# Gate projections of the last tile by seven products, with a new written order, in a fused retention and gated FFN kernel

## The chip, the cores and the metric

The kernel runs on one core of a Trainium2 chip. TensorE (PE) multiplies matrices into PSUM; VectorE (DVE), ScalarE (ACT) and GpSimd (POOL) work on rows of 128 partitions; SyncE (SP) issues transfers, and so do POOL and ACT. Each engine takes its own instructions in order and waits on semaphores for the others. The metric is device time in microseconds (us) of one execution, as a median over runs.

## The reference

```python
# retention: q, k, v of shape (4, 8, 768, 64); gamma by head
for t in range(S):
    state = gamma * state + einsum('bhd,bhe->bhde', k[:, :, t], v[:, :, t])
    y[:, :, t] = scale * einsum('bhd,bhde->bhe', q[:, :, t], state)
# x: the heads side by side, (3072, 512); d_ff is 1536
gate = 1 / (1 + exp(-(x @ w_gate)))
val = x @ w_val
out = (gate * val) @ w_out          # (3072, 512)
```

## The kernel before, in words

The sequence is cut into six tiles of 128 steps; tile t holds those steps of all four batches, 512 tokens. A *pair* P (0 to 11) is half a tile, two batches with eight heads each.

**Retention.** For a pair, `load` (line 60) fetches k, q and v through POOL's queue into buffers of four each. Pairs 0 to 3 are turned on PE (`transpose`, 171, its row 178; `turned_out`, 181, copies the result out), pairs 4 to 11 by a transposing transfer that SP issues (`xbar`, 194). `scores` (211) multiplies k and q, `mask` (219) applies the decay on DVE, `inter` (227) and `intra` (236) add the state's and the tile's own part, `y_out` (242) writes the output, transposed, into `xT`. `scaled` (200) makes decayed keys, `state` (256) their product with v. `hold` (555) and `hold_for_sums` (558) are tiny copies on POOL that keep its queue back until a pair's transposes, or a tile's hidden sums, are done. `tile_tables` (148) makes masks and decay tables of the tiles on POOL.

**Feed-forward.** The 1536 hidden columns are 12 chunks of 128, or six groups of two. `up` (297) makes one chunk of gates or values for the 512 tokens by four products of 512 columns; `up_sigmoid` (305) on ACT and `up_finish` (310) on DVE make the hidden values `hT`. Tile 1 uses halves of 256 tokens and two chunks (`up_half`, 313).

**Seven products instead of eight.** A group of two chunks, two halves of tokens and two halves of the inner dimension is a 2 x 2 by 2 x 2 block product. `half_product` (365) does it by seven block products instead of eight, each of two instructions of 256 columns, with sums of weight blocks (`ws` or `gws`) and of token blocks (`xs`, made by `x_sums`, 343, on DVE). The running sum of a bank is copied out by ACT midway (`val_copy`), and DVE adds the finished rest (`val_add`); `val_finish` multiplies with the gates on POOL and DVE. Values use this for most groups of tiles 3 and 4 and for all of tile 5. Gates do not use it in the order before, though `gate_copy`, `gate_add` and `gate_sigmoid` (412 to 427) are written. The down projection with `w_out` uses seven products too: `weight_sums` (434), `hidden_sums` (450, on DVE), `product` (464), `fast_copy`, `fast_add`, `fast_store`. `halves_sums` (333) makes the weight sums of a group by four POOL instructions, `late_weight_sums` (353) does so late, in a buffer that a load of q or k has left: before, for the sixth group of values alone.

**The order.** The kernel is scheduled by hand. `STEPS` (618) gives each step a two-letter name, and `ORDER` (678) is a list of six strings of steps, one a tile; a `+` or `-` shifts the step's tile, and a step in capitals uses the whole array in one instruction where small letters use two half-width ones (`mm`, 282). Each engine gets its instructions in this order. Names used below: `gm`, `vm` a chunk of gates or values; `gp`, `vp` one of the seven products for gates or values (first digit the group, second the product); `dw` a late weight sum (number: four times the group, plus which of the four); `hs` a hidden sum; `tp` a transposition on PE; `lk`, `lq`, `lv` loads; `xk`, `xq` turning transfers; `sc` scores; `dp` one of the seven down products. What stands ahead of `ORDER` (lines 567 to 616: the tables, pairs 0 and 1, the first chunk, and the loads up to pair 5) is issued first.

PSUM has seven banks for everything but the state (`bank`, 163). Where a buffer is taken again, the framework makes the new writer wait for the last reader.

Of the kernel before, what the change touches and what calls it, by code (L numbers as in the profile page):

```python
# [13 lines left out]
ALU = mybir.AluOpType  # L14
# [3 lines left out]
def kernel(  # L18
# [10 lines left out]
    nc = tc.nc  # L29
# [250 lines left out]
    gated = {}  # L280
# [84 lines left out]
    def half_product(t, g, n, which):  # L365
        lo, hi = (slice(i * 128, (i + 1) * 128) for i in (2 * g, 2 * g + 1))
        w, sums = ((wg, gws.get(g)), (wv, ws[:, g] if g < 5 else gws.get(6)))[which]
        mine = pairs.setdefault((t, g, which), {})
        if (n == 2) not in mine:
            mine[n == 2] = bank([128, 512])  # L370
        a = b = mine[n == 2][:, :256]
        c = mine[n == 2][:, 256:]
        for kk in range(KT // 2):
            s = lambda i: sums[:, i, kk]
            own = lambda k0, cols: w[:, k0 + kk, cols]
            x = lambda k0, c0: xT[t][:, k0 + kk, c0:c0 + 256]
            to, left, right = {
                1: lambda: (a, own(0, lo), x(0, 0)),
                2: lambda: (b, own(2, lo), x(2, 0)),
                3: lambda: (c, s(3), x(2, 256)),  # L380
                4: lambda: (a, own(2, hi), xs[t][:, 3, kk]),
                5: lambda: (c, s(0), xs[t][:, 0, kk]),
                6: lambda: (a, s(1), xs[t][:, 1, kk]),
                7: lambda: (a, s(2), xs[t][:, 2, kk]),
            }[n]()
            mm(t, to, left, right, start=(kk == 0 and n in (1, 2)), stop=(kk == KT // 2 - 1))

    def val_copy(t, g, n):
        ac = pairs[t, g, 1][0]
# [20 lines left out]
            nc.vector.tensor_tensor(h[:, 2 * g + 1, :256], s[:, :256], pairs[t, g, 1][0][:, :256], op=ALU.mult)  # L410

    def gate_copy(t, g, n):
        ac = pairs[t, g, 0][0]
        lo, hi = sigmoids(t, 2 * g), sigmoids(t, 2 * g + 1)
        o, x = {1: (lo[:, :256], ac[:, :256]), 5: (hi[:, 256:], ac[:, 256:]), 6: (lo[:, 256:], ac[:, 256:])}[n]
        nc.scalar.copy(o, x)

    def gate_add(t, g, n):
        ac, b = pairs[t, g, 0][0], pairs[t, g, 0].get(1)
        lo, hi = gated[t, 2 * g], gated[t, 2 * g + 1]  # L420
        o, x = {5: (lo[:, :256], b), 6: (lo[:, 256:], ac), 7: (hi[:, 256:], ac)}[n]
        nc.vector.tensor_tensor(o, o, x[:, :256], op=ALU.add)

    def gate_sigmoid(t, g, n):
        s = gated[t, 2 * g + (n != 6)]
        o, x = {6: (s, s), 7: (s[:, 256:], s[:, 256:]), 4: (s[:, :256], pairs[t, g, 0][0][:, :256])}[n]
        nc.scalar.activation(o, x, AX.Sigmoid)

    wt = wpool.tile([128, 4, NFF // 2, 256], BF16, name="wt")
# [183 lines left out]
    for s in range(4):  # L613
# [62 lines left out]
    }  # L676
    STEPS.update({n.upper(): f for n, f in STEPS.items()})
    ORDER = [
# [53 lines left out]
    ]  # L732
    for t, order in enumerate(ORDER):
        for s in order.split():
# [34 lines left out]
```

## Time and profile before

| what | value |
|---|---|
| median of 3 runs | 221.43 us (221.16 to 224.9) |
| span of the profiled execution, first to last instruction | 219.1 us |
| what lies around the span, median less span | 2.3 us |
| mean granted clock of TensorE | 0.992 |
| bytes moved by DMA | 25.35 MB |
| out stores on SP | 22 of 256 KB, 3.5 us to landing |

The profile was taken on one execution. A page lists busy times by engine, the chain of waits that ended last, and groups of instructions by line, with the mean duration of one and the idle time ahead of it. PE's durations overlap, since products are pipelined, so the spacing of their starts is read from the timeline. `PE position` in the text is the start of a step, if PE worked from 18.7 us on without waiting, by the spacing of the products ahead of it in the order. A row of DMA issues gives the microseconds from issue to landing.

### The profile page before, as it was taken

What the parts mean: (1) busy time and instruction counts of PE and PEld (TensorE: products, weight loads), DVE (VectorE), ACT (ScalarE), POOL (GpSimd) and SP (SyncE); (2) the same over time, 40 slices, a digit from 0 to 9 for tenths busy, and PEclk for the clock granted to TensorE, in tenths of its full rate; (3) what the DMA queues carried; (4) which work ended last, traced back from release to release, by engine and by line L of the source; (5) the groups of instructions that cost most, each with busy time, mean ns of one, the idle gap of its engine ahead of it and who ended that gap; (6) DMA issues with size and microseconds to landing.
All of it is one profiled execution on the core that took longest, in us unless ns stands there. A gap on an engine that the chain in (4) does not pass through costs nothing.

```text
span 219.1 us, 6849 instructions
## 1 busy us (share of the span) xinstructions
PE 209.3 (96%) x2900; PEld 161.2 (74%) x2906; DVE 158.3 (72%) x330; ACT 115.8 (53%) x254; POOL 131.6 (60%) x149
## 2 busy tenths in 40 slices
PE   6678999999999999999999999999999999999993
PEld 6454455889878866787689776789877867787782
DVE  6764877977448797978797688688768686474871
ACT  7484276425684373752738845635266537345431
POOL 8977786779388994699057834550083670427700
PEclk9889999999999999999999999999999999999999
DMA  9999999999991999999994999800121000022014
GB/s 127 142 171 195 192 176 159 193 191 157 144 138 51 112 183 166 167 140 152 118 215 74 180 198 168 118 0 3 57 85 56 3 1 3 0 96 79 22 46 149
DMA packets 103999, 25.35 MB, mean 116 GB/s; under 512 B 93984, under 2 KB 101152, under 8 KB 103968
## 3 DMA queue, kind: packets, MB, share of 16 engines
q0 software_dynamic: 81248, 13.90, 83.5%
q1 hardware_dynamic: 22576, 10.88, 26.6%
q8 instruction: 22, 0.36, 0.7%
q10 hardware_dynamic: 144, 0.13, 0.2%
q14 instruction: 9, 0.07, 0.1%
HBM read 28.31 MB, written 6.29 MB: 158 GB/s over the span
## 4 chain that ended last, share of the span: by engine, by line
PE 95%; DVE 2%; ACT 1%; issue 1%
PE ff L288 54%; PE ff L284 28%; PE ff L216 4%; PE ff L239 2%; PE ff L178 2%; PE ff L233 2%; PE ff L531 2%; PE z L261 1%; DVE qkT L188 1%; ACT xT L252 0%; DVE qn L572 0%; DVE xT L252 0%; ACT qkT L188 0%; DVE lgp L117 0%; ACT ob L504 0%
## 5 line engine op out<-in xcount | busy, mean ns | idle before, releaser
L308 ACT ACTIVATE gs<-ff 128x512 f32<-128x512 f32 (+1 forms) x61 | 35.2, 591 | 28.3 <-PE ff L288 17.0
L288 PE MATMUL ff<-xT,wg 128*64 128x512 bf16 (+1 forms) x408 | 47.3, 363 | 0.0
L405 POOL TENSOR_TENSOR hT<-gs,scr 128x512 bf16<-128x512 f32 x17 | 21.9, 1292 | 33.9 <-DVE scr L399 19.0
L288 PE MATMUL ff<-xT,wv 128*64 128x256 bf16 (+1 forms) x352 | 35.6, 324 | 0.0
L288 PEld LDWEIGHTS <-wg 128*64 128x64 bf16 x408 | 22.8, 110 | 11.5
L221 DVE TENSOR_TENSOR st<-ff,maskd 128x512 bf16<-128x512 f32 x40 | 25.8, 684 | 6.7 <-PE ff L216 6.6
L288 PEld LDWEIGHTS <-wv 128*64 128x64 bf16 x388 | 21.5, 110 | 7.8 <-issue 0.2
L399 DVE TENSOR_TENSOR scr<-scr,ff 128x256 f32<-128x256 f32 x51 | 20.4, 416 | 9.1 <-PE ff L284 3.5
L284 PE MATMUL ff<-xT,wg 128*128 128x256 bf16 (+1 forms) x131 | 24.3, 321 | 1.8 <-ACT xT L252 0.9
L311 DVE TENSOR_TENSOR hT<-gs,ff 128x512 bf16<-128x512 f32 (+1 forms) x27 | 17.6, 663 | 9.3 <-PE ff L288 3.9
L514 DVE TENSOR_TENSOR ob<-p,ff 128x256 f32<-128x256 f32 x33 | 13.6, 417 | 12.6 <-ACT p L506 5.5
L288 PEld LDWEIGHTS <-hT 128*64 128x64 bf16 x372 | 20.2, 110 | 2.5
L209 ACT ACTIVATE kt<-kn,tabk 128x128 bf16<-128x128 bf16 x48 | 16.9, 395 | 8.0 <-DVE hT L328 5.8
L408 POOL TENSOR_TENSOR hT<-gs,scr 128x256 bf16<-128x256 f32 x17 | 12.8, 758 | 11.3 <-DVE scr L399 8.7
L284 PEld LDWEIGHTS <-wg 128*128 128x128 bf16 x136 | 13.1, 98 | 7.7 <-issue 0.9
L254 DVE TENSOR_TENSOR xT<-ff,taby 128x512 bf16<-128x512 f32 x20 | 13.5, 686 | 3.7 <-PE ff L239 3.7
L392 ACT COPY scr<-ff 128x512 f32<-128x512 f32 x17 | 9.8, 585 | 11.8 <-PE ff L288 6.8
L288 PE MATMUL ff<-wo,hT 128*64 128x256 bf16 (+1 forms) x204 | 15.7, 292 | 0.0
L64 POOL DMA_DIRECT2D vn<-in_v_dram x12 | 14.0, 1170 | 2.4 <-DMA wo<-in_moe_w_out_dram 0.8
L284 PE MATMUL ff<-xT,wv 128*128 128x256 bf16 (+1 forms) x96 | 15.5, 290 | 0.0
L64 POOL DMA_DIRECT2D kn<-in_k_dram x11 | 13.0, 1181 | 2.7 <-PE ff L216 1.7
L288 PEld LDWEIGHTS <-hs 128*64 128x64 bf16 x252 | 13.7, 110 | 0.7
(108 smaller groups left out, 413.1 us busy)
## 6 DMA issues: line engine op xcount, KB each, us to landing
out_dram<-ob SPq DMA_DIRECT2D x22, 256.0 KB, 3.5
vn<-in_v_dram POOLq DMA_DIRECT2D x12, 256.0 KB, 10.6
kn<-in_k_dram POOLq DMA_DIRECT2D x11, 256.0 KB, 8.3
qn<-in_q_dram POOLq DMA_DIRECT2D x11, 256.0 KB, 11.1
wo<-in_moe_w_out_dram POOLq DMA_DIRECT2D x4, 384.0 KB, 12.4
wg<-in_moe_w_gate_dram POOLq DMA_DIRECT2D x5, 256.0 KB, 9.4
wv<-in_moe_w_val_dram POOLq DMA_DIRECT2D x5, 256.0 KB, 10.0
out_dram<-ob SPq DMA_DIRECT2D x3, 128.0 KB, 1.8
```

The lines of the kernel that those rows point to most:

```text
L64: nc.gpsimd.dma_start(out=held[P], in_=src(x, P))
L209: nc.scalar.activation(to[:, :, h, :], x[:, :, h, :], AX.Copy, scale=tabk[:, P // 2, h:h + 1])
L221: nc.vector.tensor_tensor(st[P, c, i], sc[P, c][i], (mask0 if P < 2 else maskd[P // 2])[:, i], op=ALU.mult)
L254: nc.vector.tensor_tensor(o, y[P, c], taby[t], op=ALU.mult)
L284: nc.tensor.matmul(o, left, right, skip_group_check=True, **kw)
L288: nc.tensor.matmul(o[half], left[:, half], right, skip_group_check=True, **kw)
L308: nc.scalar.activation(gated[t, n1][:, lo:hi], us[t, n1, 0][:, lo:hi], AX.Sigmoid)
L311: nc.vector.tensor_tensor(hidden(t)[:, n1, lo:hi], gated[t, n1][:, lo:hi], us[t, n1, 1][:, lo:hi], op=ALU.mult)
L399: nc.vector.tensor_tensor(o, o, (b if n == 5 else ac)[:, :256], op=ALU.add)
L405: nc.gpsimd.tensor_tensor(h[:, 2 * g], s, vals[t, g][:, 0:2].rearrange("p two n -> p (two n)"), op=ALU.mult)
L408: nc.gpsimd.tensor_tensor(h[:, 2 * g + 1, 256:], s[:, 256:], vals[t, g][:, 2], op=ALU.mult)
L514: nc.vector.tensor_tensor(o, x, z, op=ALU.add)
```

## The change

The gates of the last tile go by seven products. For gates, `half_product` now puts products 3 and 5 in one bank, and 2, 1, 4, 6, 7 in another, in place of product 2 alone and the rest, and opens an accumulation with whichever product comes first in a bank. Copies, additions and sigmoids follow that: three copies, two additions and three sigmoids a group. The weight sums of gate groups 0 to 5, 24 of them, are made late by POOL in old q and k buffers (`dw0` to `dw23`). All steps are written in a new order, those of tile 0 too; the steps themselves are otherwise the same.

```diff
-        if (n == 2) not in mine:
-            mine[n == 2] = bank([128, 512])
-        a = b = mine[n == 2][:, :256]
-        c = mine[n == 2][:, 256:]
+        held = n == 2 if which else n in (3, 5)
+        opens = held not in mine
+        if opens:
+            mine[held] = bank([128, 512])
+        if which:
+            b = mine[held][:, :256]
+            a, c = (mine[held][:, i:i + 256] for i in (0, 256))
+        else:
+            c = mine[held][:, :256]
+            b, a = (mine[held][:, i:i + 256] for i in (0, 256))
...
-            mm(t, to, left, right, start=(kk == 0 and n in (1, 2)), stop=(kk == KT // 2 - 1))
+            mm(t, to, left, right, start=(kk == 0 and opens), stop=(kk == KT // 2 - 1))
...
     def gate_copy(t, g, n):
...
+        o, x = {1: (lo[:, :256], False), 5: (hi[:, 256:], True), 3: (lo[:, 256:], True)}[n]
+        nc.scalar.copy(o, pairs[t, g, 0][x][:, :256] if x else pairs[t, g, 0][x][:, 256:])
...
     def gate_add(t, g, n):
...
+        o, cols = {6: (gated[t, 2 * g], slice(0, 512)),
+                   7: (gated[t, 2 * g + 1][:, 256:], slice(256, 512))}[n]
+        nc.vector.tensor_tensor(o, o, pairs[t, g, 0][False][:, cols], op=ALU.add)
...
     ORDER = [
-        "GM1 VM1 sg1 mu1 GM2 VM2 sg2 mu2 kt0 GM3 VM3 sg3 mu3 kt8 GM4 VM4 sg4 mu4 sm0 zs0 zo0 zo1 gm5 vm5 sg5 mu5  "
-        "gm6 vm6 sg6 mu6 sm1 zs1 zo2 zo3 hh0 hh1 hh2 hh3 gm7 vm7 sg7 mu7 gm8 vm8 sg8 mu8 xk4 xq4 xk5 xq5 kt16  "
-        "gm9 vm9 sg9 mu9 tp4 te4 tp5 te5 vm10 gm10 sc5 mk11 gm11 sc4 mk10 in5+ mk9 ia5+ vm11 mk8 in4+ ia4+ yo5+  "
-        "tp7+ yo4+ tp6+ sg10",
...
+        "wp1+ tt6+ VM1 kt0 aw8++ GM1 sg1 mu1 GM3 VM3 xk4 VM2 GM4 sg4 aw16++ GM2 sg2 gm7 kt8 sg3 mu2 sm0 xq4 mu3  "
+        "hh0 tt7+ hh2 gm6 gm5 sg5 zs0 zo1 wp2+ sg7 gm8 wp3+ sm1 zo0 zs1 sg8 vm8 mu8 vm6 sg6 mu6 tp4 te4 vm5 mu5  "
+        "kt16 tp5 vm7 zo3 te5 wp5+ gm11 sg11 sc4 mk8 sc5 mk10 mk11 mk9 VM4 in5+ mu4 gm10 ia5+ mu7 in4+ yo5+ hh4  "
+        "gm9 sg9 sg10 zo2 ia4+ vm11",
+        "tp6 te6 yo4 hh1- tt12+ wp6 hh5- sm2- zs2 tp7 te7 hh7- ag4 vm10- sc7 as4 kt24 wp8 sc6 sm3 mu11- in6 zo4  "
...
+        "sg9 dc04- sg4 tt11- yo12 ho7 in14 ia14 hs2 lk8 kt66 yo14 ds16- zo14 yo15 kt65 vm6 zo15 dp14- in13 ia13  "
+        "zo12 gm5 vm5 kt67 dc14- kt71 aw11 yo13 xs0+ xs2+ xs3+ xs1+ gm11 sg5 mu5 lq8 hs1 ds04-- tt13 gm6 kt68  "
...
+        "hs3- vm4- gm8- sg6- mu6- mu4- hs4- hs6- lk9- kt79 kt77 dw14+ kt73 vm8- sg10- mu10- hs5- hs7- vp1 vc15  "
+        "sg8- mu8- vm11- mu11- kt72 vp5 aw5- vp16 hs8- lq9- tt14- lv9- xk8- vc5 hs9- xq8- xk9- sc16 aw7- mk33  "
...
+        "VP54- vf46- vf56- DP11- GP11 yo22- xs0 gc01 vf54- sg9- vf47- GP05 GP15 GP22 vf44- xs2 gc05 VP1 VP5  "
+        "GP03 GP06 vf57- gc15 gc11 GP13 GP12 gc21 xs1 gc03 gc13 vc5 GP16 GP26 GP25 gc25 VP11 VP15 VP6 vc15 ga06  "
+        "GP07 GP23 hs8- DP15- VP3 VP13 gc23 ga16 gs16 xs3 GP17 ga07 GP04 VP12 ga26 GP27 ga17 dw17- hs7- VP16  "
```

In the built program PE has 470 products of 256 columns on the whole array where it had 386, and 38 of 512 columns where it had 86; the half-width ones are as many as before.

More of the change, by code (lines that the diff above doesn't have):

```diff
@@ L412, in gate_copy @@
     def gate_copy(t, g, n):
-        ac = pairs[t, g, 0][0]
         lo, hi = sigmoids(t, 2 * g), sigmoids(t, 2 * g + 1)
-        o, x = {1: (lo[:, :256], ac[:, :256]), 5: (hi[:, 256:], ac[:, 256:]), 6: (lo[:, 256:], ac[:, 256:])}[n]
-        nc.scalar.copy(o, x)
+        o, x = {1: (lo[:, :256], False), 5: (hi[:, 256:], True), 3: (lo[:, 256:], True)}[n]
+        nc.scalar.copy(o, pairs[t, g, 0][x][:, :256] if x else pairs[t, g, 0][x][:, 256:])
     def gate_add(t, g, n):
[L419 to L422, printed above, removed]
+        o, cols = {6: (gated[t, 2 * g], slice(0, 512)),
+                   7: (gated[t, 2 * g + 1][:, 256:], slice(256, 512))}[n]
+        nc.vector.tensor_tensor(o, o, pairs[t, g, 0][False][:, cols], op=ALU.add)
     def gate_sigmoid(t, g, n):
         s = gated[t, 2 * g + (n != 6)]
-        o, x = {6: (s, s), 7: (s[:, 256:], s[:, 256:]), 4: (s[:, :256], pairs[t, g, 0][0][:, :256])}[n]
+        o, x = {6: (s, s), 7: (s[:, 256:], s[:, 256:]), 4: (s[:, :256], pairs[t, g, 0][False][:, 256:])}[n]
         nc.scalar.activation(o, x, AX.Sigmoid)
```

95 rows, old and new, of the table ORDER are left out of this document.

## The prediction

> **What bounds the kernel now.** I read the page's first part, then the busy times by stretch, then the chain of work that ended last, in order of time. The page first, its busy times and the chain's shares by engine.
>
> ```profile
> span 219.1 us, 6849 instructions
> ...
> PE 209.3 (96%) x2900; PEld 161.2 (74%) x2906; DVE 158.3 (72%) x330; ACT 115.8 (53%) x254; POOL 131.6 (60%) x149
> ...
> PE 95%; DVE 2%; ACT 1%; issue 1%
> ```
>
> The busy times by stretch (first line: heading; the sum is over six stretches from 18.6 to 215.7 us), and one stretch asked for alone:
>
> ```profile
> 18.60:41.00 22.40, 22.35 (x264) 12.01 (x264) 16.57 (x24) 10.77 (x18) 17.19 (x19) 1.00 1.90 179
> ...
> 176.00:215.70 39.70, 39.38 (x310) 29.92 (x310) 26.12 (x68) 17.72 (x39) 16.27 (x16) 1.00 0.12 45
> sum 197.10, PE 196.68 PEld 150.50 DVE 145.82 ACT 103.17 POOL 116.73; mean PE 32.78 PEld 25.08 DVE 24.30 ACT 17.19 POOL 19.45
> ```
> ```profile
> 100.00:115.00 15.00, 15.00 (x267) 11.38 (x263) 13.03 (x25) 6.80 (x17) 7.01 (x10) 1.00 1.90 163
> ```
>
> The columns are length, then PE, weight loads, DVE, ACT, POOL, the granted clock and the DMA. TensorE is busy for 196.68 of 197.10 us at a clock of 1.00, and carries 95% of the chain. So only two things can move the time: the work that TensorE is given, and waits that are opened or closed on it. The stretch from 100 us shows that DVE may be busy for 13.03 of 15 us (87%) and still leave no hole in PE. The chain of waits, pieces of it (start, length, what), and PE's timeline in the last tile give the spacing of each kind of product:
>
> ```profile
> 18.70 6.87 PE ff L284 x31
> ...
> 40.96 0.89 PE ff L178 x32
> ...
> 86.88 0.25 PE z L261 x16
> ...
> 94.52 0.55 PE ff L216 x16
> ...
> 98.05 0.22 PE ff L233 x8
> ...
> 100.00 0.22 PE ff L239 x8
> ...
> 123.42 0.33 PE ff L216 x8
> ...
> 215.63 0.37 ACT ob L504
> ```
> ```profile
> 182.19 1.03 PE L284 MATMUL ff<-xT,wg 128*128 128x512 bf16 x4
> 183.05 0.38 PE L284 MATMUL ff<-xs,ws 128*128 128x256 bf16 x2
> 183.27 1.03 PE L284 MATMUL ff<-xT,wg 128*128 128x512 bf16 x4
> 184.13 0.82 PE L284 MATMUL ff<-wo,hT 128*128 128x256 bf16 x6
> 184.79 0.38 PE L284 MATMUL ff<-xT,ws 128*128 128x256 bf16 x2
> ```
>
> From start to start, four products of 512 columns take 0.86 us (0.215 each), two of 256 take 0.22 and six take 0.66 (0.11 each). From 18.70 to 215.63 us, 196.9 us, the built order holds 360 full products of 512 columns and 892 of 256 (a pair of half-width ones counted as one): 77.4 + 98.1 us. The attention products by their rows above (64 transposes, 160 scores, 320 of lines 233 and 239, 160 of line 261) are 1.8 + 5.5 + 8.8 + 2.5. Together 194.1, so some 2.8 us are waits too short for the chain to name.
>
> The span is 219.1 us and the median run 221.43, so 2.3 us lie around the span. I sum against the span and add the 2.3 back unchanged.
>
> **The change part by part.**
>
> *Gate products of the last tile.* Twelve projections of 4 x 512 columns go: 48 x 0.215 = 10.3 us. Six groups of 7 products of 2 x 256 come: 84 x 0.11 = 9.2 us. All are on PE, hence on the path: **-1.1 us**. No other product is added, though some change between whole and half-width, which cost the same by the rows.
>
> *What the gate products hang on the other engines.* These groups price it:
>
> ```profile
> L308 ACT ACTIVATE gs<-ff 128x512 f32<-128x512 f32 x59 | 34.4, 598 | 27.7 <-PE ff L288 17.0 <-PE ff L284 10.4
> ...
> L399 DVE TENSOR_TENSOR scr<-scr,ff 128x256 f32<-128x256 f32 x51 | 20.4, 416 | 9.1 <-PE ff L284 3.5 <-ACT scr L394 2.6 <-ACT scr L392 1.5
> ...
> L339 POOL TENSOR_TENSOR ws<-wv 128x256 bf16<-128x256 bf16 x10 | 7.0, 716 | 0.0
> ...
> L152 POOL TENSOR_SCALAR_AFFINE_SELECT maskd<-tabk 128x512 f32<-128x512 f32 x10 | 6.3, 640 | 6.6 <-DVE st L221 6.6
> ...
> L394 ACT COPY scr<-ff 128x256 f32<-128x256 f32 x17 | 6.2, 374 | 6.5 <-PE ff L288 4.4 <-PE ff L284 1.9
> ...
> L270 DVE TENSOR_TENSOR za<-za,z 128x512 f32<-128x512 f32 x8 | 5.4, 681 | 0.1
> ...
> L443 POOL TENSOR_TENSOR scr<-wo 128x512 f32<-128x512 bf16 x3 | 3.5, 1152 | 3.5 <-ACT wt L446 3.5
> ```
>
> ACT loses 12 sigmoids of 0.598 and gets 18 copies of 0.374, 6 sigmoids of 0.598 and 12 half-size ones, which no row after the start shows; the copy of the same size is the nearest, 0.374. Net 6.7 + 3.6 + 4.5 - 7.2 = +7.6 us. DVE gets 6 additions of 0.681 and 6 of 0.416: +6.6 us. In the last 39.7 us ACT goes from 17.7 to 25.3 us, 66% of a stretch shortened by 1.1, and is covered. DVE goes from 26.1 to 32.7 of 38.6, 85%: what hides it is the rest of DVE's idle time. Its cost lies between nothing (87% from 100 us on cost PE nothing) and all 6.6 us (every addition waited for). It is nearest to the first row; but here additions come several within one product and PSUM banks wait for them, so I take **+0.5 us**.
>
> *Gate weight sums.* 24 GpSimd operations of 0.716 us, 17.2 us, spread over tiles 1 to 5. Five of them stand in the last tile's order. GpSimd has 131.6 of 219.1 us busy, so they fit; what waits behind them on its queue are hidden products and loads. A sum needs weights alone, so nothing but the queue holds it. The shortest distances in PE work between its place in the order and its product are 1.7 us (the fourth sum of value group 5, in tile 4), then 6 us. Taken at nothing, up to the 3.6 us of five sums if they hold the queue. They sit in q and k buffers, so loads of pairs 8 to 11 have two q buffers instead of four, and wait for the transposes two pairs before them. Each such load already stands behind a hold on POOL that waits for a later transpose, so nothing new waits.
>
> *Tile 0 in a new order.* Twenty projections (0.86 each, by the 6.87 us that 32 of their products take in the chain), three state products, six pieces of scores and outputs and three transposes of 0.445 now stand ahead of the q transposes of pair 3: 17.2 + 0.8 + 1.4 + 1.3 = 20.7 us after 18.7, so PE wants q of pair 3 at 39.4 us. Its load is issued by POOL, whose order up to there is unchanged, and lands as the queue's row says:
>
> ```profile
> 28.00 1.14 POOL L64 DMA_DIRECT2D qn<-in_q_dram  x1 [0.22 <-issue]
> ```
> ```profile
> qn<-in_q_dram POOLq DMA_DIRECT2D x1, 256.0 KB, 12.5
> ```
>
> 28.0 + 12.5 = 40.5. The kernel before reaches these transposes at 40.96 and waits for nothing; the new one waits 1.1, of which I take **+1.0 us** for what else may be late there (0 if that load comes a microsecond sooner, 2 if as much later). Late next are the up projections behind them, by the same amount.
>
> *Loads, transposes and stores that move.* From pair 6 on, k and q are loaded on POOL, turned by a DMA that SP issues, and read by scores on PE. The tightest of the near ones is pair 6:
>
> ```profile
> 81.01 3.51 SPq L197 DMA_TRANSPOSE qkT<-qn  x1
> ```
> ```profile
> qkT<-qn SPq DMA_TRANSPOSE x1, 9.4
> ```
>
> It landed at 90.4, and its scores ran at 94.5: 4.1 us to spare. They now stand at PE position 89.7, near 91 us with tile 0's wait, which leaves 0.7. On SP one store fewer is ahead of it; on POOL seven more operations (five weight sums of 0.716, one mask of 0.640 and one sum of w_out of 1.152: 5.4 us) are ahead of its load. What covers them are POOL's own waits there (its list of waits):
>
> ```profile
> POOL scr L443 <- ACT wt L446: 3.5, 1, 3.5
> ...
> POOL kept L556 <- DMA qkT<-qn: 3.2, 2, 1.6
> POOL kept L559 <- DVE hs L460: 3.0, 1, 3.0
> ```
>
> The first and half of the second, 5.1 us, lie ahead of this load. Taken at nothing, with up to 2 us if a wait for ACT stays. Pairs 7, 9, 10 and 11 keep 2 us or more by the same count; pair 8 is a rival.
>
> *The other tiles in a new order.* What may be gained or lost is the 2.8 us of short waits: from -2.8 (all closed) to +2.8 (twice as many). Walking both built orders with the prices above, I count the PE waits whose own producer (the DVE or ACT operation on a finished product) has 0.3 us or less to spare between the start of tile 1 and the end of tile 4: six before, three in the new order. I take **-0.6 us**, and both ends for the range.
>
> Sum: 219.1 - 1.1 + 0.5 + 1.0 - 0.6 = 218.9, and with 2.3 around it **221.2 us**.
>
> **A rule against the change.** Two rows of DVE's timeline, two hidden sums beside GpSimd work and one alone:
>
> ```profile
> 79.12 2.77 DVE L460 TENSOR_TENSOR hs<-hT 128x512 bf16<-128x512 bf16 x2
> ...
> 85.68 0.42 DVE L460 TENSOR_TENSOR hs<-hT 128x512 bf16<-128x512 bf16 x1
> ```
>
> Alone such a sum takes 0.42 us; the two that met a GpSimd operation took 2.77 together. The Trainium skill (SBUF — State Buffer, Who interferes with whom) states that a DVE instruction with both inputs in SBUF and a GpSimd instruction that reads SBUF lock each other out, the later one blocked to the end of the first. By that rule the trace agrees, and each late gate sum may hold a DVE sum for its whole length. It is part of the second rival.
>
> **The rivals.**
>
> *First: the new order closes most of the short waits* (to 219.0 - 220.3 us). For it: fewer tight pairs from tile 1 to 4. Against it: the wait of tile 0 is added, and near-zero spare times remain at the end. With 2.2 of the 2.8 us closed instead of 0.6: 221.2 - 1.6 = 219.6.
>
> *Second: DVE becomes the bound of the last tile* (222.2 - 224 us). The 85% above, and the five late sums of 0.716 that may each hold one of the tile's sums: 3.6 us of hold would bring DVE to 36.3 of 38.6, 94%. If half of the hold and 0.4 more of queueing reach PE: 221.2 + 1.8 + 0.4 = 223.4. Against it: the 87% stretch without loss.
>
> *Third, slower: the turned q of pair 8 comes late.* Its first scores are moved from 123.4 us (the row of eight scores above) to PE position 112.6, about 113.6 us with tile 0's wait. SP issued that transpose here:
>
> ```profile
> 99.83 1.67 SPq L197 DMA_TRANSPOSE qkT<-qn  x1
> ```
> ```profile
> qkT<-qn SPq DMA_TRANSPOSE x1, 10.0
> ```
>
> It landed at 109.8. A spare of 13.6 us shrinks to 3.8. On POOL 6.8 us more work than before, five gate sums (3.6 us) in it, now stand ahead of the load of pair 8, and on SP four stores ahead of the transpose. It decides from 3.8 us of delay on. The cover are POOL's three waits quoted above, 9.7 us, all ahead of this load. If none of it helps, 6.8 - 3.8 = 3.0 us of wait, 224.2 us; if the stores hold the transpose another 3 us, 227.2.
>
> That the change would not do what it says is no rival: the built program has 48 fewer products of 512 columns and 84 more of 256.
>
> **How the numbers follow.** Forecast, 220.3 to 222.2: 0.50. First rival: 0.22. Second: 0.17. Third: 0.10. Something else: 0.01. The range 219.4 to 224.0 leaves out about 0.07 of the first rival and 0.07 of the second and third. About 2%, 4.4 us, is what a measurement of this kernel can tell from no change. Faster than 217.0 would need the products' gain, every short wait and no cost at all: 0.01. Slower than 225.9 is the third rival's far end: 0.04. The rest, 0.95, is within.
>
> **What the new profile would show.** Right: about 3072 fewer columns on PE, worth 1.1 us; a wait of PE for DMA qn near 39.5 us; DVE at 80 to 90% after 176 us with PE over 98% busy. Wrong: PE waiting for the turned q near 113 us (third rival); DVE over 92% and holes in PE after 176 us (second); PE reaching the transposes of pair 3 without a wait, or the last product ending before 214 us (first).

## The result, and the profile after

The changed kernel takes 223.91 us (median of 6 runs, 222.1 to 229.16) against 221.3 for the kernel before on the same chip: 1.0106 times as long, 95% interval 1.0071 to 1.0141. The forecast was 221.2. The profiled execution has a span of 222.1 us, 3.0 more than before; around it lie 1.7 us, 0.6 less than the 2.3 that the prediction added back, so the span missed its forecast of 218.9 by 3.2 us and the time by 2.7. Executions over 1.5% above the fastest of their kernel are left out of the ratios, which leaves two runs each for E6, E7 and E8, and the profiles of E3 to E7 and E11 are of such executions, so they show what can happen and not what a ratio is made of. First the page: span, busy times, and the chain's shares by engine.

```profile
span 222.1 us, 7001 instructions
...
PE 209.0 (94%) x2942; PEld 164.6 (74%) x2942; DVE 167.0 (75%) x342; ACT 121.2 (55%) x278; POOL 147.9 (67%) x173
...
PE 76%; DMA 11%; POOL 5%; DVE 4%; issue 1%; ACT 1%; DVEq 0%; POOLq 0%; ACTq 0%
```

PE's busy time hardly moved (209.3 before), its share of the chain fell from 95% to 76%: PE waits, and the chain runs through a load, GpSimd and DVE. The busy times by stretch say where (columns as in the prediction):

```profile
18.60:41.00 22.40, 21.89 (x288) 11.91 (x288) 15.17 (x26) 10.98 (x18) 17.02 (x19) 1.00 1.89 179
41.00:76.00 35.00, 35.00 (x544) 30.18 (x540) 24.95 (x41) 18.07 (x39) 31.55 (x35) 1.00 1.46 134
76.00:110.00 34.00, 32.32 (x532) 24.34 (x528) 30.65 (x53) 23.25 (x58) 25.86 (x31) 1.00 1.70 161
110.00:142.00 32.00, 30.90 (x496) 24.07 (x494) 21.65 (x45) 13.11 (x28) 17.48 (x20) 1.00 1.58 142
142.00:176.00 34.00, 34.00 (x564) 27.76 (x562) 27.81 (x63) 17.23 (x35) 21.45 (x27) 1.00 0.11 34
```
```profile
176.00:216.00 40.00, 39.87 (x376) 34.23 (x373) 33.39 (x83) 25.59 (x67) 19.52 (x21) 1.00 0.11 41
```

PE is full except in three stretches: 0.5 us are missing in tile 0, 1.7 from 76 us on, 1.1 from 110 us on. The last tile, where the products are, is full at 39.87 of 40 us, with DVE at 83%. PE's list of waits names the same three:

```profile
PE ff L288 <- DVE xT L254: 1.7, 1, 1.7
...
PE ff L288 <- DVE ob L518: 1.1, 1, 1.1
...
PE ff L288 <- DMA wg<-in_moe_w_gate_dram: 0.4, 1, 0.4
```

Setting each product's start against the spacing of all products ahead of it gives the waiting in full, the short waits too: from 18.7 us to the last product 2.75 us before and 6.71 after. To 42 us it is 0.0 and 1.5; from 42 to 78 us 0.5 and 0.5; to 84 us 0.1 and 1.8; to 126 us 1.0 and 0.6; to 132 us 0.4 and 1.3; to 174 us 0.2 and 0.4; in the last tile 0.5 and 0.6. So 4.0 us of waiting came and 1.1 us of work went. The chain's pieces (start, length, what) show the three places. In tile 0:

```profile
21.18 11.26 DMA qn<-in_q_dram
...
32.48 0.64 PE ff L178 x16
```

PE reaches the transposes of q of pair 2 before the load has landed; ahead of that it had waited for the gate weights of chunk 7 (24.95 us) and for k of pair 2 (30.85 us). At 82 us:

```profile
73.66 2.48 DVE st L221 x4
76.15 0.61 DVE hT L328
...
76.78 2.06 DVE hs L464 x3
...
78.86 0.79 DVE hs L464
...
79.66 1.73 DVE hs L464
81.39 0.60 DVE za L270
81.99 0.61 DVE xT L254
...
82.64 1.46 PE ff L288 x17
```

PE waits for the bank that the eviction of pair 5 (`xT`) empties. The eviction stands in DVE's queue behind five hidden sums (`hs`), which take 4.6 us in place of 2.1 at 0.42 each. GpSimd's timeline beside them:

```profile
77.72 0.82 POOL L339 TENSOR_TENSOR qn<-qn,wg 128x256 bf16<-128x256 bf16 x1
78.51 0.80 POOL L152 TENSOR_SCALAR_AFFINE_SELECT maskd<-tabk 128x512 f32<-128x512 f32 x1
79.29 0.86 POOL L339 TENSOR_TENSOR ws<-wv 128x256 bf16<-128x256 bf16 x1
80.12 0.66 POOL L339 TENSOR_TENSOR qn<-wg 128x256 bf16<-128x256 bf16 x1
```

Each of the later sums ends some 0.3 to 0.6 us after a GpSimd operation does; the one of 1.73 us lasts through two. And at 130 us:

```profile
124.52 0.43 DVE ob L518
...
124.97 4.75 DMA out_dram<-ob
...
129.85 0.43 DVE ob L518
...
130.32 3.84 PE ff L288 x43
```

An addition of a down product waits for an output buffer (`ob`, four of them) whose store was issued 3 us before it, and PE waits for the addition. A buffer is short because the new order stores the second rows of tile 1 (`ds04`) only in tile 4's string; its data is there in tile 2's.

### The profile page after: what moved, and what is told of

It reads as the page before. It is cut to its first block, busy times and chain, and to the rows that moved or that the text cites. A ratio compares the mean times of both kernels' runs of the same rounds, so it can differ in the third digit from the quotient of the medians.

```text
span 222.1 us, 7001 instructions
## 1 busy us (share of the span) xinstructions
PE 209.0 (94%) x2942; PEld 164.6 (74%) x2942; DVE 167.0 (75%) x342; ACT 121.2 (55%) x278; POOL 147.9 (67%) x173
## 4 chain that ended last, share of the span: by engine, by line
PE 76%; DMA 11%; POOL 5%; DVE 4%; issue 1%; ACT 1%; DVEq 0%; POOLq 0%; ACTq 0%
PE ff L288 45%; PE ff L284 23%; DMA qn<-in_q_dram 5%; DMA wg<-in_moe_w_gate_dram 4%; PE ff L216 2%; DMA out_dram<-ob 2%; DVE hs L464 2%; PE ff L233 2%; PE ff L239 2%; DVE st L221 1%; POOL kn L64 1%; POOL vn L64 1%; PE z L261 1%; PE ff L178 1%; POOL wg L85 1%
## 5 line engine op out<-in xcount | busy, mean ns | idle before, releaser
L308 ACT ACTIVATE gs<-ff 128x512 f32<-128x512 f32 (+1 forms) x49 | 28.3, 587 | 29.2 <-PE ff L288 23.3
L288 PE MATMUL ff<-xT,wv 128*64 128x512 bf16 (+1 forms) x352 | 35.0, 324 | 0.0
L414 POOL TENSOR_TENSOR hT<-gs,scr 128x256 bf16<-128x256 f32 x17 | 12.3, 729 | 16.3 <-ACT p L510 6.9
L284 PE MATMUL ff<-xT,wg 128*128 128x256 bf16 (+1 forms) x112 | 16.5, 288 | 1.6 <-ACT xT L252 1.0
L284 PEld LDWEIGHTS <-wg 128*128 128x128 bf16 x124 | 12.0, 98 | 5.2 <-issue 1.2
L328 DVE TENSOR_TENSOR hT<-gs,ff 128x512 bf16<-128x512 f32 x12 | 8.1, 685 | 8.1 <-ACT gs L324 4.8
L64 POOL DMA_DIRECT2D qn<-in_q_dram x11 | 12.8, 1164 | 1.2 <-issue 0.5
```

The lines of the kernel that those rows point to most:

```text
L64: nc.gpsimd.dma_start(out=held[P], in_=src(x, P))
L284: nc.tensor.matmul(o, left, right, skip_group_check=True, **kw)
L288: nc.tensor.matmul(o[half], left[:, half], right, skip_group_check=True, **kw)
L308: nc.scalar.activation(gated[t, n1][:, lo:hi], us[t, n1, 0][:, lo:hi], AX.Sigmoid)
L328: nc.vector.tensor_tensor(hidden(t)[:, n1:n1 + 2, lo:lo + 256], gated[t, n1, half], us[t, n1, half, 1], op=ALU.mult)
L414: nc.gpsimd.tensor_tensor(h[:, 2 * g + 1, 256:], s[:, 256:], vals[t, g][:, 2], op=ALU.mult)
```

## The experiments

All times below are against runs of the kernel before on the same chip, as a ratio with its 95% interval.

**E1, the old order up to tile 4 with the new last tile.** The strings of tiles 0 to 4 are those before; I put the gate sums between their steps.

```diff
+ (tile 3) gm5 dw0+ ... gm10 dw1+ ... gm2 dw2+ ...    (tile 4) gm0 dw16 ... vp3 dw8 ... gm3 dw9 ...
+ (tile 5) va57- VP44- yo23- GP01 GP02 GP21 hs4- hs1- hs3- hs5- hs6- VP54- ...
```

> The strings of tiles 0 to 4 as before, the last tile as changed (gates by seven products), and the late gate sums put between the steps of tiles 3 and 4. Theory A (the time came from three waits that the new order opens ahead of the last tile: some 1.2 us in tile 0, 1.9 at 82 us, 1.3 at 130 us, while the products give their 1.1): none of the three waits is here, so the span is 219.1 - 1.1 + 0.3 = 218.3 us, 0.8 below the kernel before. Theory B (the gate products and their sums cost what they save, by DVE and ACT in the last tile or by GpSimd operations that hold DVE): 219.1 us or more, no faster than before.

Measured: 1.0303 (1.0285 to 1.0322). By the number that is theory B's side, but far beyond what B priced. To 132 us PE waits 2.5 us, where it waited 2.0 in the kernel before; then 8.6 us come, on waits for `scr`, `hs` and, 2.2 us at 185 us, for `xs`, behind the five hidden sums that I had put ahead of it. So it can't tell what the products are worth; it tells that GpSimd sums and hidden sums are not free wherever they are put.

**E2, the new order up to tile 4 with the old last tile**, without the 24 gate sums.

```diff
- ... dw0++ ... dw23- ...  GP01+ GP02+ GP21+ ...
+ (tile 5) VP12 vf56- GM0 vf46- ... sg0 ... GM11
```

> The new strings of tiles 0 to 4 without the 24 gate sums and the three gate products in them, and the last tile as before (gates by full projections). Theory A: the three waits stay, and the 1.1 us of the products are lost: 222.1 + 1.1 - 0.3 = 222.9 us, or up to 0.8 less where the two gate sums that are gone at 78 and 80 us let the hidden sums on DVE pass sooner. Theory B: without products and sums the time falls to 219 to 220 us.

Measured: 1.0159 (1.0136 to 1.0182), against 1.0106 with the products: the last tile's change with all that hangs on it is worth 0.53%, 1.2 us, though the intervals overlap by a hair. Two of the three waits are there without it (the first was 1.7 us with the gate sums):

```profile
PE ff L288 <- DVE xT L254: 1.1, 1, 1.1
PE ff L288 <- DVE ob L518: 1.0, 1, 1.0
```

Theory A holds, B falls.

**E3, the store early.**

```diff
- (tile 4) gm7 ds04--- vf17
+ (tile 2) dc04- ds04- sg4
```

> The changed kernel with one store moved: that of the second rows of tile 1 (its data is ready in tile 2's string) from tile 4's string to the place right behind its copy in tile 2's. Theory C (this store, left to tile 4, keeps one of the four output buffers, so an addition of tile 2's down product has to wait at 128 us for a store that was issued 3 us before): the wait of DVE for the store (1.8 us) and that of PE for the addition (1.1) are gone, 222.1 - 1.3 = 220.8 us. Rival (the store lands late because loads fill the transfer engines there, and any store is late): the wait stays in part, 221.5 to 222.1 us.

Measured: 1.0047 (1.003 to 1.0065), 0.59% or 1.3 us less than the changed kernel, as theory C has it; the two intervals don't overlap. DVE's addition, later in this execution, no longer waits for a store (between brackets the idle time ahead and what ended it):

```profile
132.19 0.42 DVE L518 TENSOR_TENSOR ob<-p,ff 128x256 f32<-128x256 f32 x1 [0.34 <-PE ff L288]
```

But SP, which takes its transfers in order, stood before that store until its data came, and the turning transfers of pair 8 behind it were issued from 106.8 us on, though the load of k had landed at 98.8:

```profile
105.41 0.33 SPq L526 DMA_DIRECT2D out_dram<-ob  x1
...
106.83 2.17 SPq L197 DMA_TRANSPOSE qkT<-kn  x1
```

**E4, evictions ahead of the hidden sums.**

```diff
- hs4- hs5- dt3-- ... zs4- kt47- yo10- yo11- dp15-
+ zs4- yo10- yo11- hs4- hs5- dt3-- ... kt47- dp15-
```

> The changed kernel with the state sum and the two output evictions of pair 5 moved ahead of the hidden sums that stand before them in tile 2's string; nothing else. Theory D (DVE takes five hidden sums ahead of the evictions, four of which wait for GpSimd, 0.77 to 1.73 us in place of 0.42, and PE's bank comes free late): PE's wait of 1.7 us at 81 us is gone, 222.1 - 1.8 = 220.3 us. Rival (the hidden sums, now 2 us later, are waited for by the down products instead): 221.5 us or more, with PE waiting for hs or hT near 82 to 86 us.

Measured: 1.0137 (1.0109 to 1.0165), no gain. The wait changed its name, as the rival said. Of the two waits below, the one of 2.4 us is at 83.3 us, where the rival puts it; the other, 1.4 us at 80.5, stands in E3's profile too, where these steps are as in the changed kernel:

```profile
PE ff L288 <- DVE hs L464: 3.8, 2, 2.4
```

**E5, a quiet GpSimd.** DVE's order stays; GpSimd is held by a tiny copy that reads the second eviction.

```diff
+    def hold_for_x(t, n):
+        nc.gpsimd.tensor_copy(kept[:, 3:4], xT[t][:, 0, n:n + 1])
...
- dw13+++ ... tt10- ... aw10 ... dw2++ ... aw9 ... yo10- yo11- dp15-
+ yo10- yo11- hx511 tt10- aw10 dw2++ dw13++ aw9 dp15-
```

> The changed kernel with DVE's order untouched: two gate sums, two value sums and a mask of GpSimd that stand at 77 to 82 us are put behind a tiny copy on GpSimd that waits for the second output eviction of pair 5. Theory E (the GpSimd operations hold DVE's hidden sums, and that makes the eviction late): the five hidden sums ahead of it take 0.42 to 0.5 us each (2.1 to 2.5 in all, 4.5 before), the eviction comes 2 us sooner, PE's wait of 1.7 us is gone, 222.1 - 1.8 = 220.3 us. Rival (DVE has too much in its queue there, whatever GpSimd does): the sums stay over 0.7 us each, or the wait stays, 221.8 us or more.

Measured: 1.0015 (0.9967 to 1.0063), 0.9% or 2.0 us less than the changed kernel, and the intervals don't overlap. DVE's timeline shows the same five sums:

```profile
80.90 1.10 DVE L464 TENSOR_TENSOR hs<-hT 128x512 bf16<-128x512 bf16 x3
82.03 0.43 DVE L464 TENSOR_TENSOR hs<-hs,hT 128x512 bf16<-128x512 bf16 x1
82.49 0.43 DVE L464 TENSOR_TENSOR hs<-hT,hs 128x512 bf16<-128x512 bf16 x1
```

They take 2.0 us in all, and PE's wait there is gone. Theory E holds. In this execution, though, PE waited 2.6 us at 52 us, where the edit changes nothing. DVE, then GpSimd, there:

```profile
47.81 3.69 DVE L464 TENSOR_TENSOR hs<-hT,hs 128x256 bf16<-128x256 bf16 x1
51.43 1.27 DVE L254 TENSOR_TENSOR xT<-ff,taby 128x512 bf16<-128x512 f32 x2
```
```profile
47.65 1.25 POOL L447 TENSOR_TENSOR scr<-wo 128x512 f32<-128x512 bf16 x1
48.87 0.63 POOL L152 TENSOR_SCALAR_AFFINE_SELECT maskd<-tabk 128x512 f32<-128x512 f32 x1
49.48 1.28 POOL L339 TENSOR_TENSOR ws<-wv 128x256 bf16<-128x256 bf16 x2
50.72 0.63 POOL L152 TENSOR_SCALAR_AFFINE_SELECT maskd<-tabk 128x512 f32<-128x512 f32 x1
```

In the changed kernel's profile this sum came 1.9 us sooner, ahead of the first of these operations:

```profile
45.89 0.28 DVE L464 TENSOR_TENSOR hs<-hT,hs 128x256 bf16<-128x256 bf16 x1
```

A second place, then, at which a microsecond or two decide whether a sum takes 0.28 us or 3.69.

**E6, tile 0's transposes later.** The main moves; five projections behind them (`VM4`, `gm9` to `gm11`, `vm11`) change places too.

```diff
- sg2 gm7 kt8 ... gm6 gm5 sg5 zs0 ...  sg6 mu6 tp4 te4 vm5 mu5 kt16 tp5 vm7 ...
+ sg2 kt8 ... gm6 gm5 sg5 gm7 zs0 ...  sg6 mu6 vm5 mu5 tp4 te4 vm7 kt16 gm9 sg9 tp5 ...
- (tile 1) zs2 tp7 te7 hh7- ag4 vm10- sc7
+ (tile 1) zs2 vm10- tp7 te7 hh7- ag4 sc7
```

> The changed kernel with tile 0's steps put in the order in which its loads land: gates of chunk 7 behind those of 5 and 6, the transposes of pair 2 and of q of pair 3 behind one or two more projections. Theory A: PE's three waits for loads at 24.9, 30.9 and 32.5 us, 1.2 us in all, shrink to 0.2 at q of pair 3 (landing at 40.5 us): 222.1 - 1.0 = 221.1 us. Rival (the loads give the pace, and whatever is gained there is lost at q of pair 3): 222.0 us.

Measured: 1.01 (1.0046 to 1.0154), no gain that can be told. In the profile the waits for loads went from 1.4 to 0.2 us, but 1.1 us came back at 42 to 44 us, at what stands behind the transposes, and at the second place above PE waited 3.15 us (to 51.55 us). The pieces at 42 to 44 us:

```profile
42.40 0.62 PE L216 MATMUL ff<-qkT 64*128 64x128 bf16 x16 [0.23 <-ACT qkT L188]
43.23 0.44 PE L261 MATMUL z<-vn,kt 128*64 128x64 bf16 x16 [0.22 <-DVE kt L206]
```

**E7, the three edits in one** (E3, E5 and E6).

> The three edits in one: the early store, the quiet GpSimd and the later transposes of tile 0. If the three waits are all that the order opened, and they don't hide each other: 222.1 - 1.3 - 1.8 - 1.0 = 218.0 us of span, 1.1 below the kernel before. Rival (one wait's mending opens the next): 219 us or more, no better than before.

Measured: 1.0065 (1.0002 to 1.0128). The rival's side: the two large waits of the profile are the second place and the turned q of pair 8, whose transfer stood behind the moved store on SP, went out at 111.0 us and took 12.0 us beside loads on GpSimd's queue.

```profile
51.81 1.92 PE L288 MATMUL ff<-xT,wg 128*64 128x256 bf16 x16 [3.20 <-DVE xT L254]
```
```profile
123.17 0.40 PE L216 MATMUL ff<-qkT 64*128 64x128 bf16 x8 [2.25 <-DMA qkT<-qn]
```

**E8, no gate sums.** The gates of the last tile are made with the value weights' sums, so its output differs from the reference.

```diff
-        w, sums = ((wg, gws.get(g)), ...
+        w, sums = ((wg, ws[:, g] if g < 5 else gws.get(6)), ...
```

> The changed kernel without the 24 sums of gate weights; the gate products read the sums of the value weights instead, so the gates of the last tile are not those of the reference. Theory E (GpSimd sums cost by holding DVE): two of the sums stood at 78 and 80 us, PE's wait there shrinks by some 0.8 us, and the last tile loses its 0.3: 221.0 us. Rival (the sums lie in GpSimd's idle time, as the prediction has it): 222.1 us.

Measured: 1.0095 (1.0041 to 1.015), the same as with them within a wide interval, and 222.1 us of span in the profile: the rival by the number. PE's waits there:

```profile
PE ff L288 <- DVE ob L518: 1.6, 1, 1.6
...
PE ff L288 <- DVE xT L254: 1.2, 1, 1.2
```

The wait at 82 us is 0.5 us shorter than with the two gate sums, part of what theory E says; the rest stays, since a mask and value sums of GpSimd run beside the hidden sums there in any case. The wait for the output buffer is 0.5 us longer. So the 24 sums as placed cost nothing net that can be told.

**E9, store behind the turning transfer, quiet GpSimd, and two sums of tile 1 behind the evictions.**

```diff
- (tile 1) ag6 hh6- av6 ... av4 hh3- wp7 ... yo6 yo7 BG2
+ (tile 1) ag6 av6 ... av4 wp7 ... yo6 yo7 hh6- hh3- BG2
+ (tile 3) xq8- ds04-- xk9-
```

> The changed kernel with three edits: the quiet GpSimd of the run before; the store of tile 1's second rows put behind the turning transfer of pair 8's q in tile 3's string (in tile 2's string it had held that transfer back on SP); and, in tile 1, two hidden sums of DVE put behind the evictions of pair 3, so that no eviction stands behind a sum that can meet a run of GpSimd operations there. Theory F (sums of DVE that meet runs of GpSimd operations, and one store left too late, are what the order costs, tile 0 apart): no wait of PE over 0.5 us between 45 and 200 us, 222.1 - 1.8 - 1.3 = 219.0 us in every execution, and fewer executions that are far longer. Rival (the order is tight everywhere, each mending opens another wait): over 220 us, or a wait of 1 us or more at a new place.

Measured: 1.0042 (1.0021 to 1.0062), and the 12 runs lie between 221.8 and 223.26. The waits at 82 and 130 us are gone, but the span of 220.3 us is on the rival's side, and one wait of over 0.5 us is left from 45 to 200 us: 1.8 us at 52 us, for what now stood behind the same sum on DVE, a sum that the edit had itself put beside GpSimd's run:

```profile
47.79 3.69 DVE L464 TENSOR_TENSOR hs<-hT,hs 128x256 bf16<-128x256 bf16 x1
```

**E10, the same with the old tile 0** and tile 1's head fitted to it.

> The same with tile 0's string of the kernel before, and the head of tile 1's string fitted to it. Theory A: the 1.2 us that tile 0 lost to loads come back, 217.8 us, 1.3 below the kernel before. Rival (what tile 0 did ahead of time has to be done in tile 1, where DVE is full from 36 to 42 us): 219 us or more, with PE waiting for st, hT or kt near 42 to 46 us, as in the run with tile 0's transposes moved.

Measured: 0.9982 (0.9961 to 1.0004), 219.8 us of span in the profile. Nothing is lost to 36 us; of it 0.9 us come back at 45.5 us on the state product (`kt`), 0.5 at 47.2 (`st`) and 0.7 at 92.6 (turned q of pair 6). For the larger part that is the rival, and the interval does not tell it from the kernel before; against E9 the old tile 0 gives 0.60%, 1.3 us, as theory A has it.

**E11, E9 with the sums at 55 us**, where GpSimd pauses.

```diff
- yo6 yo7 hh6- hh3- BG2 ... kt36 hh8- hh9-
+ yo6 yo7 BG2 ... kt36 hh6- hh3- hh8- hh9-
```

> The kernel of three edits (early store, quiet GpSimd, two hidden sums of tile 1 behind the evictions) with those two sums put still further back, from 46 us to 55 us, where GpSimd has a pause of 2 us. Theory F: at 47.8 us one of them took 3.69 us, as long as five GpSimd operations ran without a pause, and PE waited 1.8 us for what stood behind it on DVE; at 55 us both take under 1.3 us, and the time falls by 1.8 to 2.0 us, to 218.4 us. Rival (a hidden sum that is waited for, or DVE full whatever stands there): 219.5 us or more.

Measured: 0.9961 (0.9929 to 0.9993), median 220.67. The profiled execution lost 3.9 us ahead of 36 us, on the first loads and copies, so only what follows is read from it: the sums take 0.28 us each at 57 us, and PE has no wait of over 0.3 us from there on. Against E9 the time fell by 0.81%, 1.8 us, as forecast. Theory F holds.

**E12, the same with the old tile 0.**

```diff
- sc7 kt24 wp8 sc6 sm3 in6 ... mk12 ia6 aw12+ mk15 in7
+ sc7 wp8 sc6 in6 ... mk12 ag6 ia6 aw12+ mk15 kt24 in7 ... BG2 sm3 BG0
- (tile 2) sc13 kt62 sc12 dp07-
+ (tile 2) dp07- sc13 kt62 sc12
```

> The kernel with the old string of tile 0, likewise with its hidden sums at 55 us; besides, the keys' scaling of pair 3 behind the masks and its state product later (PE waited 0.9 and 0.5 us there), and one down product ahead of the scores of pair 6 (PE waited 0.7 us for the turned q). Theory: 219.2 - 0.9 - 0.5 - 0.6 = 217.2 us. Rival (what is moved is waited for elsewhere): 218.5 to 219.5 us, the same as before.

Measured: 0.9972 (0.9947 to 0.9997), median 220.32 against 221.07: 0.3% faster than the kernel before, its interval just clear of 1, and not to be told from E10 or E11. That is the rival's number, 218.4 us of span in the profile; two of the moved sums ran beside GpSimd again, 1.25 and 1.24 us each, though PE did not wait for them. Span, busy times, the chain's shares:

```profile
span 218.4 us, 7016 instructions
...
PE 208.3 (95%) x2942; PEld 165.7 (76%) x2942; DVE 169.6 (78%) x342; ACT 121.9 (56%) x278; POOL 148.9 (68%) x174
...
PE 90%; DMA 5%; DVE 2%; ACT 1%; issue 0%; SPq 0%
```

With the same steps as the changed kernel and one tiny copy on GpSimd more, PE waits 3.1 us from 18.7 us on, where that waited 6.7 and the kernel before 2.75. E11 and E12, with the waits mended, are 0.9 and 0.6 us faster than the kernel before, with intervals of some 0.7 and 0.6 us to either side, so the 1.1 us that the products were to give fits.

## Why the prediction was wrong

The step that failed is "The other tiles in a new order", -0.6 us. It is +2.4: from 42 to 174 us the waiting grew from 2.2 to 4.6 us, by 1.7 at 82 us and 0.9 at 130 us. It counted the waits whose own producer has little time to spare, with each DVE operation at the price of one that stands alone. Two things escaped it. First, what stands ahead of a producer on DVE: five hidden sums, which beside GpSimd cost 4.6 us in place of 2.1. The row of 2.77 us for two such sums and the rule behind it stood in the prediction, but were put to the late gate sums alone, in the last tile. E5 shows that GpSimd's computing operations are the cause (the same sums take 2.0 us beside its DMA issues). E8 and E2 show that the gate sums are a part of it: without them PE's wait is 1.2 and 1.1 us in place of 1.7. Second, the output buffers: the step on "Loads, transposes and stores that move" followed the turned keys and queries and not how long a moved store keeps its buffer. E3 puts 1.3 us on that one store.

That 223.9 us lies inside the stated range, and in the band of the second rival (222.2 to 224), is luck: what that rival describes did not happen.

The other steps:
- *Gate products*, -1.1: right as far as shown; E2 gives -1.2, net of what they hang on the other engines.
- *What they hang on other engines*, +0.5: about 0.1. DVE's share was forecast at 85% and is 83%, PE stays full, and one wait of 0.3 us at 205 us is all that shows. The second rival fell.
- *Gate sums at nothing*: right as placed, net and within E8's interval; E1 shows it isn't so in any place.
- *Tile 0*, +1.0: mis-sized, 1.5, and not by the wait that it named. The landing of q of pair 3 was right (40.5 us), but PE did not wait for it. Overlooked was that weights and pair 2 are wanted ahead of their landing too; having waited there, PE reaches pair 3 just behind its load, at 40.67 us. In E6's profile most of what was mended here came back at 42 to 44 us.
- *Pair 6*, 0.7 us to spare: 2.7 in the changed kernel, where q landed at 90.35 us as before and PE came at 93.04, 2 us later than reckoned. In E10, where q landed at 92.45, PE waited 0.7.
- *The third rival*, q of pair 8: landed 111.6 us, wanted at 116.2, no wait. Its mechanism, a transfer made late by what is put ahead of it on SP, is real: in E7 it costs 2.25 us.
- *The first rival* fell with the failed step.

The sum as measured: 219.1 - 1.1 + 0.1 + 1.5 + 2.4 = 222.0, against 222.1.

## What to carry to other kernels

In a hand-written order, price what stands ahead of a producer on its engine, not the producer alone, and price sums of two SBUF operands on DVE by the GpSimd work that can run beside them. Keep DVE operations on the critical path out of reach of back-to-back GpSimd work, or hold GpSimd with a copy that reads what must come first. When a store is moved, look both at how long its buffer is kept and at what waits behind it on its queue.

## What the runs showed of the hardware

A DVE sum of 256 columns with both operands in SBUF took 0.28 us alone and 3.69 us beside five GpSimd operations without a pause between them (E5, E6, E7, E9). The Trainium skill (SBUF — State Buffer, Who interferes with whom) says that the later of the two is blocked to the end of the first; here the sum did not get in between one GpSimd operation and the next at four such ends, so a price of one operation is too low. It got in at the fifth end, though a sixth operation followed there without a pause; why there, the runs don't show. In E3 a sum of 512 columns took 3.24 us beside four such operations, though by the profile it had started 0.34 us ahead of the first. DMA issues of GpSimd, 1.15 us each, did not hold the sums (three in 1.10 us at 80.90, E5). Over the profiles of all fourteen kernels, 481 sums of 512 columns beside no GpSimd work took 0.41 to 0.43 us each, 68 beside DMA issues alone took the same but for one of 0.85, and 271 beside computing operations alone had a median of 0.67 us.

A long hole can cost more than its length. E7's busy times by stretch around its wait at 51.8 us:

```profile
48.60:51.80 3.20, 0.01 (x1) 0.00 (x0) 3.20 (x3) 0.00 (x0) 3.20 (x5) 0.84 2.43 157
51.80:57.50 5.70, 5.69 (x54) 5.69 (x55) 2.07 (x4) 1.89 (x4) 3.27 (x4) 0.50 2.42 143
```

After 3.2 us of idle PE the granted clock was 0.50 for 5.7 us, which adds some 2.8 us to the loss (an estimate, half of the 5.7). In E6 a hole of 3.15 us at the same place left the clock at 1.00; in E3 holes of 1.4, 0.4 and 2.1 us within 5 us were followed by a granted clock of 0.57 from 86 to 90 us. The Trainium skill (TensorE: Matmul & The Clock Gate, Part 1: The HAM clock gate) has a free-running window of 3.4 us over which activity is judged; a hole that trips it in one execution and not in another agrees with that, though the holes after which the clock fell here are shorter than that window. The clock does not account for the spread of the runs: two of E7's, both with a mean granted clock of 0.992, took 221.85 and 228.26 us.
